# A hand-written order of events, set anew on all five engines, with 270 zero products in place of 390

## The chip, the cores and the metric

The kernel runs on one core of a Trainium2 chip. A core has five engines that each work through their own stream of instructions in order: PE (TensorE, the matrix multiplications), DVE (VectorE), ACT (ScalarE), POOL (GpSimd) and SP (SyncE, which here only issues the DMAs). The engines wait for each other through semaphores. The metric is the time of one execution in microseconds (us) on the device, the median of the runs shown; a profile is one execution more, with a record of every instruction.

## What is computed

A recurrent attention (a delta rule) over 32 independent heads, then a feed-forward network on its output:

```python
B, H, S, D = 4, 8, 768, 48
k_n = k / (np.linalg.norm(k, axis=-1, keepdims=True) + 1e-06)
for t in range(S):
    y[:, :, t] = q_t @ state
    v_old = state^T @ k_n_t
    state = state + beta_t * outer(k_n_t, v_t - v_old)
x = y.transpose(0, 2, 1, 3).reshape(3072, 384)
h = x @ w_in                        # 384 x 2048
g = h * erf(softplus(h))
out = g @ w_out                     # 2048 x 384
```

## The kernel before

**Attention.** The 768 steps are cut into 12 chunks of 64. For each chunk `c` the kernel forms products of keys with keys (`gram_mm ... pg`, masked and scaled in `gram_a`) and of keys with queries (`gram_mm ... pq`, `gram_p`). A triangular system has to be solved for each chunk: the matrix goes to DRAM and back in another layout (`to_dram`, `to_blocks`), 31 rows are eliminated one after the other (`solve_row`, two instructions each, L316 and L318), two chunks at a time; the result goes back through DRAM (`put_blocks`, `from_blocks2`) and is completed by two small products (`merge_t`, `merge_e`, `merge_z`, `merge_m`). The first solve (chunks 0 and 1) runs on DVE, the five others on POOL. Then four recurrences (one per batch entry `b`, index `j = 4c + b`) run through the chunks: `chain_u` on PE, `chain_u2` on DVE, then `chain_s` and `chain_y` on PE, `chain_s2` on DVE, `chain_y2` on ACT.

**Feed-forward.** The output of every chunk makes one group `g` of 256 tokens, so there are 12 groups. The values are scaled and split in two 16-bit parts (`x_max`, `x_all`, `x_scale`, `x_tr`, `x_hi`, `x_lo`), and so are the weights (`w_load`, `w_mask`, `w_sign`, `w_bits`, `w_sum`, then `w_max`, `w_all`, `w_scale`, `w_hi`, `w_lo`, and for `w_in` `w_lo1` on PE and `w_lo2` on ACT). A group has 16 `ffn1` (nine matmuls of 256 columns each, L632), eight units of softplus, erf, product and split (`e_sp`, `e_erf` on ACT, `e_mul` on DVE, `e_split`, `e_rest`), and 16 `ffn2` (six matmuls of 384 columns, L687 to L689). Softplus and erf sit in two table sets of ACT. Where an event needs another set than the event before it in the order, `table` writes a table load (L138).

**Zero products.** `warm` multiplies a tile of zeros by itself, 384 columns, into a bank that nothing reads. `fill` is one such product. 15 are issued at the start, and `WU` more are events of their own.

**What sets the order.** Every call such as `on(us(19), load_q, 0)` puts one event in a list. The list is sorted by the planned time, and then `ORDER`, a tuple written out by hand, picks the events one by one. The instructions of each engine are issued in exactly that order; the scheduler is set to manual for all five engines. An event that isn't ready holds up everything behind it on its engine. So the order on each engine can be read out of the tuple alone.

Around the first solve that gives on PE, before the change: 15 zero products, 5 more, `gram_mm` (1,1,pg), 36 more, three `gram_mm`, 108 more, four `gram_mm` (pq), 7 more, `gram_mm` (2,0,pg), 234 more, `gram_mm` (2,1,pg), `w_all` of `w_in`, `merge_e` of chunk 0. On DVE: the gram products, six `w_sign` and five `w_bits`, the norms of chunks 2 and 3, the 31 solve rows with 10 `w_sign` and 6 `w_bits` between them, four `w_bits`, `gram_a` (2,0), `gram_p` (0,0), `w_max`, `gram_a` (2,1), `merge_t` of chunk 0. SP issues `put_blocks` and `from_blocks2` of both chunks when the solve is done.

Of the kernel before, what the change touches and what calls it, by code (L numbers as in the profile page):

```python
# [11 lines left out]
ALU = mybir.AluOpType  # L12
# [25 lines left out]
C2 = 12.0  # L38
C3 = 16.0
SS2 = 12.8  # L40
S1 = -2.5
SPL = 32
WG = -6
WU = 390
MT = 58
M1 = 0
WL = (0.9, 0.95, 1.0, 1.05, 1.1, 1.15, 24, 24.1, 31.0, 32.5, 34.0, 35.5)
WK = (6.0, 6.7, 7.4, 8.1, 8.8, 9.5, 28, 29, 36.0, 37.5, 39.0, 40.5)
WF = (6.6, 7.3, 8.0, 8.7, 9.4, 10.1, 28.6, 29.6, 36.6, 38.1, 39.6, 41.1)
WI = (17.0, 18.0, 19.0, 20.0, 21.0, 22.0, 31, 32, 50.5, 52.1, 53.7, 55.3)  # L50
# [32 lines left out]
def delta_ffn_kernel(ctx, tc, kT, qT, ktok, vtok, btok, w_in, w_out, cst, out):  # L83
    nc = tc.nc
    te, ve, se, ge, sp = nc.tensor, nc.vector, nc.scalar, nc.gpsimd, nc.sync
# [18 lines left out]
    def on(t, fn, *a, **kw):  # L104
        ev.append((t, len(ev), lambda: fn(*a, **kw)))

    def us(x):
        return (x - T0) / SW
# [279 lines left out]
    ygrp, mg = {}, {}  # L388
# [54 lines left out]
    def chain_y2(j):  # L443
        g, js = divmod(j, GS)
        if js == 0:
            ygrp[g] = []
            mg[g] = sm.tile([P, GS], F32, tag="mg", name=f"mg{g}")
        y = at.tile([P, NP * D], F32, tag="y", bufs=YR, name=f"y{j}")
        ygrp[g].append(y)
        se.copy(y, pcs[j][0][:, :192])  # L450
# [13 lines left out]
    def stage(nm, i, n=RW):  # L464

        return wb[nm].rearrange("p a b -> p (a b)")[:, DM + i * n:DM + i * n + n]
# [32 lines left out]
    def w_bits(nm, i, k):  # L499
        raw = wt[nm]["raw", i]  # L500
        ai = stage(nm, i).bitcast(I32)
        if k == 0:
            ve.scalar_tensor_tensor(ai, ai, 3, raw[:, :, 0], op0=ALU.logical_shift_left, op1=ALU.bitwise_or)
# [202 lines left out]
    def chain_at(j):  # L706
        if j < B:
            return us(MT + 8.3 + 2 * j)
        if j < 2 * B:
            return us(MT + 17 + 2 * (j - B))  # L710
        if j < 3 * B:
            return C2 + 1.2 * (j - 2 * B)
        if j < 4 * B:
            return C3 + 1.2 * (j - 3 * B)
        return j * NFF * SF / GS - NFF * SF - LEAD
# [29 lines left out]
    on(-98, warm, WARM)  # L745
    for i in range(WU):
        on(us(6 + 0.17 * i), fill)
# [8 lines left out]
    for sg in range(2):  # L756
        t = (4, 20)[sg]
# [13 lines left out]
    for c in range(4):  # L771
        t = (5.5, 8, 63.2, 65.2)[c]
# [10 lines left out]
    for c in range(2):  # L783
        for i in range(2):
            t = (56, 57, 71.5, 73)[2 * c + i]
# [3 lines left out]
    for sg in range(NSG):  # L789
# [7 lines left out]
        for s0 in range(31):  # L797
            t = t0 + (t1 - t0) * s0 / 31
# [39 lines left out]
    for j in range(B * NC_):  # L838
        t = chain_at(j)
        d = 1.0 if j >= 2 * B else 2.6 / SW / CS  # L840
        on(t - 3.3 if j >= 2 * B else us(32 + 2 * j) if j < 6 else t - us(6) + us(0), load_v, j)
        on(t - 1.2 if j >= 2 * B else us(52 + 1.3 * j) if j < 6 else t - us(2) + us(0), put_v, j)
        on(t, chain_u, j)
        on(t + 0.2 * d, chain_u2, j)
        if j < B * NC_ - B:
            on(t + CS * d, chain_s, j)
            on(t + (CS + 0.25) * d, chain_s2, j)
        on(t + (CS + 0.05) * d, chain_y, j)
        on(t + (CS + 0.3) * d, chain_y2, j)
        on(t + (CS + 0.7) * d, chain_m, j)  # L850


    for i, (tl, tk, tf, tb) in enumerate(zip(WL, WK, WF, WI)):
        on(us(tl), w_load, "in", w_in.bitcast(I32), i, RI[i])
        on(us(tk), w_mask, "in", i)
        on(us(tf), w_sign, "in", i)
        for k in range(2):
            on(us(tb + 0.8 * k), w_bits, "in", i, k)
        on(us(tb + 2.4), w_sum, "in", i)
    for i in range(NRW):  # L860
        t = us(WOT[i])
        on(t - 0.9, w_load, "out", w_out.bitcast(I32), i, RO[i])
        on(t - 0.3, w_mask, "out", i)
        on(t - 0.2, w_sign, "out", i)
        for k in range(2):
            on(t + 0.15 * k, w_bits, "out", i, k)
        on(t + 0.5, w_sum, "out", i)
# [52 lines left out]
    ev.sort(key=lambda e: (e[0], e[1]))  # L920
    if ORDER:
        ev = [ev[i] for i in ORDER]
    E = mybir.EngineType
# [45 lines left out]
```

## Time and profile before

| what | value |
|---|---|
| three runs | 699.67, 704.69 and 709.21 us, median 704.69 |
| profiled execution, its own time | 704.84 us |
| span of its instructions | 703.1 us |
| mean granted clock of TensorE | 0.977 |
| PE busy | 674.4 us, of which 69.9 are the 405 zero products |
| ACT busy | 542.9 us, of which 234.8 are 183 table loads |
| DVE and POOL busy | 424.3 and 307.6 us |

The span runs from the first to the last instruction; the execution's own time has 1.74 us around it. Matmuls are pipelined: the record of one lasts longer than the pace at which they follow one another (405 records of 337 ns on the mean, but 69.9 us of busy time). "PEclk" in a row is the granted clock of TensorE as a share of full speed.

### The profile page before, as it was taken

To read this page: it belongs to the slowest core of one execution; us is meant where nothing else is said; L and a number is where in the kernel's file an instruction comes from. 1 tells how busy PE (TensorE), PEld (TensorE's weight loads), DVE (VectorE), ACT (ScalarE), POOL (GpSimd) and SP (SyncE) were. 2 spreads that over 40 slices of the span, in tenths; PEclk is the share of its full clock that TensorE was granted. 3 is DMA by queue.
4 is the path that set the end of the run, shared out by engine and by line. 5 is a ranking of instruction groups with operands and counts; after the bars stand their busy time and mean duration, and the time that the engine had idled before them with its cause. 6 is when DMAs were issued, how large, how long until landed. Compare 5 with 4: busy or idle time off the path is not lost.

```text
span 703.1 us, 22184 instructions
## 1 busy us (share of the span) xinstructions
PE 674.4 (96%) x9473; PEld 509.3 (72%) x9473; DVE 424.3 (60%) x976; ACT 542.9 (77%) x767; POOL 307.6 (44%) x492
## 2 busy tenths in 40 slices
PE   8999888899999999999999999999999999999997
PEld 4666575666777777777786877777777778777764
DVE  3769586696656975568665668565554645534321
ACT  7333234998998599879688796798897897899994
POOL 2012004798379718981276851288612131111111
PEclk9999968999999999999999999999999999999999
DMA  9692539403633166123461152521230400101000
GB/s 319 152 296 86 121 91 275 119 1 91 132 64 82 24 154 138 35 60 80 92 158 25 37 132 46 106 60 33 49 91 12 82 14 2 25 1 25 1 23 22
DMA packets 87395, 59.05 MB, mean 84 GB/s; under 512 B 67776, under 2 KB 77120, under 8 KB 87296
## 3 DMA queue, kind: packets, MB, share of 16 engines
q1 hardware_dynamic: 87296, 57.63, 32.9%
q8 instruction: 74, 1.21, 0.7%
q14 instruction: 25, 0.20, 0.1%
HBM read 43.45 MB, written 14.16 MB: 82 GB/s over the span
## 4 chain that ended last, share of the span: by engine, by line
PE 68%; ACT 15%; DVE 10%; issue 3%; DMA 2%; SPq 1%; ACTq 0%; DVEq 0%
PE ph L632 19%; PE warm L153 9%; PE pr L687 7%; ACT L138 7%; PE pr L689 6%; PE pr L688 6%; PE pq L255 3%; PE pc L441 3%; PE pg L255 3%; PE pc L414 3%; ACT L L659 2%; ACT L L654 2%; PE pc L427 2%; DVE z L435 2%; PE pr L558 1%
## 5 line engine op out<-in xcount | busy, mean ns | idle before, releaser
L138 ACT ACT_TABLE_LOAD x183 | 234.8, 1283 | 4.0 <-PEq L962 0.7
L632 PE MATMUL ph<-xh,w_in 128*128 128x256 f16 x1152 | 219.2, 275 | 4.1 <-DVE L L663 4.0
L632 PEld LDWEIGHTS <-w_in 128*128 128x128 f16 x1728 | 167.2, 99 | 42.8 <-issue 6.6
L676 POOL TENSOR_TENSOR H<-L,H 128x512 f16<-128x512 f32 x58 | 67.4, 1163 | 213.9 <-DVE H L672 144.2
L632 PE MATMUL ph<-xl,w_in 128*128 128x256 f16 x576 | 158.4, 275 | 0.0
L687 PE MATMUL pr<-w_out,H 128*128 128x384 f16 x384 | 125.7, 327 | 0.0
L689 PE MATMUL pr<-w_out,H 128*128 128x384 f16 x384 | 125.4, 326 | 0.0
L688 PE MATMUL pr<-w_out,H 128*128 128x384 f16 x384 | 125.3, 326 | 0.0
L663 DVE SCALAR_TENSOR_TENSOR L<-ph,L 128x512 f32<-128x512 f32 x96 | 65.8, 686 | 84.5 <-ACT L L659 83.8
L401 POOL TENSOR_TENSOR z<-v,nm 64x192 f32<-64x192 f32 x96 | 50.8, 529 | 101.3 <-DMA v<-vtok 54.9
L316 POOL TENSOR_TENSOR tmptmpg<-gb,xb 128x31 f32<-128x31 f32 (+15 forms) x155 | 82.9, 535 | 24.1 <-DMA gb<-d 15.1
L318 POOL TENSOR_TENSOR xb<-xb,tmptmpg 128x31 f32<-128x31 f32 (+15 forms) x155 | 86.7, 559 | 12.2
L654 ACT ACTIVATE L<-ph,xct 128x512 f32<-128x512 f32 x96 | 66.0, 687 | 17.6 <-PE ph L632 14.5
L153 PE MATMUL warm<-zero 128*128 128x384 f16 x405 | 69.9, 337 | 1.1 <-DVE zero L144 1.1
L153 PEld LDWEIGHTS <-zero 128*128 128x128 f16 x405 | 40.3, 101 | 29.1 <-issue 3.4
L659 ACT ACTIVATE L<-L 128x512 f32<-128x512 f32 x96 | 60.3, 630 | 1.0
L689 PEld LDWEIGHTS <-H 128*128 128x128 f16 x384 | 37.5, 98 | 24.9
L687 PEld LDWEIGHTS <-H 128*128 128x128 f16 x384 | 37.5, 98 | 17.5
L420 DVE TENSOR_TENSOR z<-pc,ga 64x192 f32<-64x192 f32 x88 | 31.2, 354 | 29.9 <-PE pc L414 25.1
L688 PEld LDWEIGHTS <-H 128*128 128x128 f16 x384 | 37.6, 98 | 15.6
L670 ACT CAST H<-L 128x512 f16<-128x512 f32 x56 | 34.3, 614 | 17.1 <-DVE L L663 16.8
L435 DVE TENSOR_TENSOR z<-pc,z 48x192 f32<-48x192 f32 x80 | 28.2, 352 | 28.1 <-PE pc L441 27.2
(139 smaller groups left out, 948.0 us busy)
## 6 DMA issues: line engine op xcount, KB each, us to landing
raw_in<-w_in SPq DMA_DIRECT2D x12, 512.0 KB, 7.0
raw_out<-w_out SPq DMA_DIRECT2D x12, 512.0 KB, 5.9
d<-A SPq DMA_DIRECT2D x22, 256.0 KB, 3.1
k<-ktok SPq DMA_DIRECT2D x12, 384.0 KB, 4.9
kpg<-kT SPq DMA_DIRECT2D x24, 192.0 KB, 4.9
qp<-qT SPq DMA_DIRECT2D x24, 192.0 KB, 4.0
v<-vtok SPq DMA_DIRECT2D x48, 96.0 KB, 2.6
out<-ob SPq DMA_DIRECT2D x48, 96.0 KB, 2.2
```

The lines of the kernel that those rows point to most:

```text
L138: se.add_instruction(mybir.InstLoadActFuncSet(name=nc.get_next_instruction_name(), act_func_set_id=i, ins=[], outs=[]))
L153: te.matmul(wp[0], zero[:, :P], zero, start=True, stop=True)
L316: eng.tensor_tensor(tv, G[:, s, s + 1:].unsqueeze(1).broadcast_to([P, ncol, nr]), Xv[:, :, s:s + 1].broadcast_to([P, ncol, nr]), op=ALU.mult)
L318: eng.tensor_tensor(Xv[:, :, s + 1:], Xv[:, :, s + 1:], tv, op=ALU.add)
L632: te.matmul(ph, w[:, i, kt * P:kt * P + P], G[x][:, :, ksl], start=(m == 0), stop=(m == 8))
L654: se.activation(unit(g, u), G["ph", u], AF.Softplus, bias=0.0, scale=G["ct"])
L659: se.activation(Lu, Lu, AF.Erf, bias=0.0, scale=1.0)
L663: ve.scalar_tensor_tensor(Lu, fg[g]["ph", u], HSC, Lu, op0=ALU.mult, op1=ALU.mult)
L676: (ve if u % (2 if g < GLE else GLM) == 0 else ge).tensor_tensor(G["gl", u], unit(g, u), G["gh", u], op=ALU.subtract)
L687: te.matmul(G["po"][a], gh[:, o, asl], wout_h[:, i, :], start=(i == 0), stop=False)
L688: te.matmul(G["po"][a], gh[:, o, asl], wout_l[:, i, :], start=False, stop=False)
L689: te.matmul(G["po"][a], gl[:, o, asl], wout_h[:, i, :], start=False, stop=(i == NFF - 1))
```

## The change

`WU` goes from 390 to 270, so 120 of the zero products fall away. `ORDER` is another permutation of all the events: on each engine nearly every event has another neighbour. `chain_y2` is rewritten so that the members of a group can come in any order, and the second, empty call of `w_bits` is dropped from the list (it issued nothing). No other instruction is added or taken away by hand; the number of table loads follows from the order.

```diff
-ORDER = (0,1,3,4,2,27,5,6,7,8,9,12,10,11,22,24,13,25,28,30,14,60,15,236,34,
...
+ORDER = (0,1,2,12,7,21,22,24,25,28,30,34,36,37,40,42,44,45,49,51,33,27,3,5,
...
-WU = 390
+WU = 270
...
-        if js == 0:
-            ygrp[g] = []
+        if g not in ygrp:
+            ygrp[g] = {}
...
-        ygrp[g].append(y)
+        ygrp[g][js] = y
...
-    def w_bits(nm, i, k):
+    def w_bits(nm, i):
...
-        if k == 0:
-            ve.scalar_tensor_tensor(ai, ai, 3, raw[:, :, 0], op0=ALU.logical_shift_left, op1=ALU.bitwise_or)
+        ve.scalar_tensor_tensor(ai, ai, 3, raw[:, :, 0], op0=ALU.logical_shift_left, op1=ALU.bitwise_or)
```

The new tuple, read out as the order on each engine up to the first feed-forward work (F and a number: so many zero products; `s` a `solve_row`):

```
PE    warm 15, pg(0,0), F14, pg(0,1), pg(1,0), pg(1,1), F133, pq(1,1), F7,
      pq(0,1), pq(0,0), F21, pg(2,0), pq(1,0), F69, pg(2,1), pg(3,1), F18,
      merge_e 0, F5, merge_z 0, merge_e 1, chain_u 0, pg(3,0), merge_z 1,
      chain_u 1, chain_y 0, merge_m(1,1), chain_s 0, merge_m(1,0), chain_s 1,
      chain_u 2, chain_u 3, w_all in, chain_y 1, chain_s 2, chain_y 3,
      chain_y 2, chain_s 3, chain_u 5, x_tr(0,0), F3, w_lo1 0, chain_y 5,
      w_lo1 1, 2, 3, x_all 0, w_lo1 4, chain_s 5, chain_u 4, w_lo1 5,
      x_tr(0,1), w_lo1 6, pq(2,0), w_lo1 7, ffn1 2, 0, 1, ...
DVE   norm_sum 2, 0, 1, norms of chunks 0 and 1, norm_sum 3, gram_a(0,0),
      gram_a(0,1), w_sign x2, w_bits, gram_a(1,0), gram_a(1,1), then 5 w_sign,
      6 w_bits and the norms of chunks 2 and 3, s0 to s30 with 11 w_sign and
      5 w_bits between them, w_ident, gram_p(1,1), gram_p(1,0), w_sign x2,
      w_bits x2, gram_a(2,0), gram_a(2,1), merge_t 0, gram_p(0,1),
      merge_e2(0,0), merge_t 1, gram_p(0,0), merge_z2(0,0), ...
SP    kT 0, k 1, beta 0, k 2, k 0, w in8, kT 1, w out0, k 3, w out2, in2, in1,
      out11, in4, to_dram 0, 1, to_blocks 0, beta 1, to_blocks 1, w in5, in7,
      in0, out3, out1, q 1, w out10, v 0, q 0, w in6, kT 2, w in10, cst,
      from_blocks 0, w in11, in9, in3, out5, kT 3, w out6, v 2, kT 2, w out4,
      put_blocks 0, 1, from_blocks 1, v 1, from_blocks2 0, 1, ...
```

After that the order goes on as before in kind, with the two `ffn1` of a unit next to each other, the softplus of a unit often set directly ahead of another unit's, and the feed-forward work of a group spread over a longer stretch. Counted over the whole tuple, the ACT order switches its table set 147 times, where the old one switches 183 times.

More of the change, by code (lines that the diff above doesn't have):

```diff
@@ L856, in delta_ffn_kernel @@
         on(us(tf), w_sign, "in", i)
-        for k in range(2):
-            on(us(tb + 0.8 * k), w_bits, "in", i, k)
+        on(us(tb), w_bits, "in", i)
         on(us(tb + 2.4), w_sum, "in", i)
@@ L864, in delta_ffn_kernel @@
         on(t - 0.2, w_sign, "out", i)
-        for k in range(2):
-            on(t + 0.15 * k, w_bits, "out", i, k)
+        on(t, w_bits, "out", i)
         on(t + 0.5, w_sum, "out", i)
```

2 lines of the change are left out of this document (1 added, 1 removed).

## The prediction, made before the changed kernel was run

> **What bounds the kernel now.** I read the busy shares first, then busy time by stage, then the timeline where a stage has holes.
>
> ```profile
> span 703.1 us, 22184 instructions
> PE 674.4 (96%) x9473; PEld 509.3 (72%) x9473; DVE 424.3 (60%) x976; ACT 542.9 (77%) x767; POOL 307.6 (44%) x492
> L138 ACT ACT_TABLE_LOAD x183 | 234.8, 1283 | 4.0 <-PEq L962 0.7
> L153 PE MATMUL warm<-zero 128*128 128x384 f16 x405 | 69.9, 337 | 1.1 <-DVE zero L144 1.1
> ...
> 0.00:86.10 86.10, 81.23 (x729) 51.10 (x730) 56.74 (x149) 32.48 (x63) 13.15 (x24) 0.98 0.67 194
> 86.10:160.00 73.90, 61.61 (x1072) 47.80 (x1073) 57.65 (x139) 51.59 (x107) 38.86 (x60) 0.83 0.46 121
> 160.00:698.00 538.00, 531.59 (x7676) 410.37 (x7674) 309.45 (x690) 458.80 (x598) 255.61 (x409) 1.00 0.27 61
> 698.00:703.10 5.10, 0.00 (x0) 0.00 (x0) 0.48 (x1) 0.00 (x0) 0.00 (x0) 0.90 0.32 77
> ```
>
> The columns of the stage rows are: stage, length, busy time of PE, weight loads, DVE, ACT and POOL, granted clock, DMA share, GB/s. From 160 to 698 us PE is busy 531.59 of 538 at full clock, with work that the change keeps: at most 6.4 us can be gained there, whatever the other engines do. What can be won lies before 160. Up to 86.1 us PE is busy too, but 69.9 of 81.23 us are zero products; the work that counts there is the first solve on DVE. From 86.1 to 160 PE has 12.3 us of holes and a clock of 0.83.
>
> ```profile
> 18.73 0.69 DVE L265 TENSOR_TENSOR A<-pg,gn 128x512 f32<-128x512 f32 x1 [2.28 <-PE pg L255]
> 21.21 0.68 DVE L265 TENSOR_TENSOR w_out<-pr,gn 128x512 f32<-128x512 f32 x1
> 33.17 0.19 DVE L316 TENSOR_TENSOR tmpT<-gb,xb 128x31 f32<-128x31 f32 x1
> 47.76 0.43 DVE L497 TENSOR_SCALAR raw_out<-raw_out 128x512 int32<-128x512 int32 x1 [3.73 <-DMA raw_out<-w_out]
> 51.54 0.43 DVE L497 TENSOR_SCALAR raw_out<-raw_out 128x512 int32<-128x512 int32 x1 [0.91 <-DMA raw_out<-w_out]
> 70.88 0.21 DVE L318 TENSOR_TENSOR xb<-xb,tmpT 128x31 f32<-128x31 f32 x1
> 71.12 1.09 SPq L323 DMA_DIRECT2D d<-xb  x2
> 74.20 4.30 SPq L338 DMA_DIRECT2D xm<-d  x8
> xm<-d SPq DMA_DIRECT2D x48, 64.0 KB, 2.4
> 44.34 38.20 PE L153 MATMUL warm<-zero 128*128 128x384 f16 x234
> 82.47 1.15 PE L255 MATMUL pg<-kpg 48*64 48x64 f32 x32
> 83.66 0.69 DVE L265 TENSOR_TENSOR A<-pg,gn 128x512 f32<-128x512 f32 x1 [8.08 <-PE pg L255]
> 84.27 1.42 DVE L345 STREAM_TRANSPOSE T<-xm 32x512 f32<-32x512 f32 x2
> 86.07 1.20 PE L353 MATMUL pe<-T,A 32*32 32x32 f32 x64 [1.17 <-DVE m_in L520]
> ```
>
> The solve runs from 33.17 to 71.09. Its result leaves at 71.12, and the loads back into `xm` are issued from 74.20 on, chunk 0 in the first half of the 4.30 us, so chunk 0 is there at about 74.20 + 2.15 + 2.4 = 78.75. But `merge_t` (L345) starts at 84.27: on DVE it stands behind `gram_a` (2,1), which waited 8.08 us for a `gram_mm` that stood behind 234 zero products on PE, done at 82.5. So **the zero products have become the end of the stage**: they hold the merge by 84.27 - 78.75 = 5.5 us.
>
> **The change part by part.**
>
> *Fewer zero products ahead of the merge.* The old order has 390 and the 15 of the start ahead of `merge_e` 0, the new one 262 and the 15. One costs 38.20/234 = 0.163 us, so the queue ahead of the merge is 128 x 0.163 = 20.9 us shorter. This isn't the gain: the solve's end then decides. What becomes of the 5.5 us: in the new order the last gram products of chunks 2 and 3 are followed by 18 zero products, 2.9 us. If the keys of chunk 3 land by 60 us, as the DMA order allows, PE is through at about 66, and the hold is gone: -5.5. Bound on the other side: 0, if PE's queue is late again.
>
> *An earlier start of the solve.* The last `gram_a` ahead of the solve began at 21.21, after a wait of 2.28 for a `gram_mm` behind 36 zero products, and after six `w_sign` and a `w_bits`. In the new order `gram_mm` (0,0) comes first, and two `w_sign` and one `w_bits` stand in between; against that, one more norm sum stands ahead (I allow 1 us). I get 20.4 for the end, against 21.89. Behind it DVE has 5 `w_sign`, 6 `w_bits` and 18 norm instructions:
>
> ```profile
> 15.69 0.76 DVE L497 TENSOR_SCALAR raw_in<-raw_in 128x512 int32<-128x512 int32 x2
> 22.47 3.10 DVE L503 SCALAR_TENSOR_TENSOR w_in<-w_in,raw_in 128x512 int32<-128x512 int32 x5
> 29.00 0.18 DVE L215 TENSOR_SCALAR n<-n 128x32 f32<-128x32 f32 x1
> L316 DVE TENSOR_TENSOR tmpT<-gb,xb 128x31 f32<-128x31 f32 (+15 forms) x31 | 11.5, 372 | 0.8
> L318 DVE TENSOR_TENSOR xb<-xb,tmpT 128x31 f32<-128x31 f32 (+15 forms) x31 | 11.4, 368 | 1.1
> ```
>
> 5 x 0.38 + 6 x 0.62 + (33.17 - 29.00) = 9.8, so the solve starts at about 30.3, 2.9 earlier. (The trip of the matrix through DRAM took at most 33.17 - 21.89 = 11.3 before; if it takes that, 31.7.)
>
> *A solve with fewer waits.* Rows: 11.5 + 11.4 + 1.9 between instructions = 24.8. Before there were 10 `w_sign` and 6 `w_bits` in it and 4.6 us of waits for weights (3.73 + 0.91); 37.9 in all. The new order has 11 and 5, which is about the same work. Its waits I bound from 0 to 5: the SP order has `w in6` stuck until ACT has freed a buffer, and ACT stands in `w_mask` of out10, which SP loads after out3 and out1; so `w in3` comes late, by my count about 1 us after DVE needs it. I take 1.3, so -3.3. The solve then ends near 30.3 + 37.9 - 3.3 = 64.9, and `merge_e` 0 begins at about 64.9 + 7.6 (the trip back, as 78.75 against 71.12) + 1.5 = 74.0, in place of 86.07: **-12.1 us**, bounds -17 and -6.
>
> *From the merge to the first softplus.*
>
> ```profile
> 134.82 0.69 ACT L654 ACTIVATE L<-ph,xct 128x512 f32<-128x512 f32 x1
> 89.86 0.68 DVE L358 COPY T<-pe 32x512 f32<-32x512 f32 x1
> 127.06 1.09 DVE L620 SCALAR_TENSOR_TENSOR xl<-pt,xsx,xh 128x256 f16<-128x256 f32 x3 [0.24 <-ACT xh L615]
> 89.86:128.15 38.29, 32.84 (x713) 27.06 (x713) 28.88 (x69) 18.40 (x43) 9.98 (x22) 0.76 0.70 185
> 134.80:160.00 25.20, 21.07 (x215) 14.41 (x213) 20.00 (x52) 24.88 (x50) 22.77 (x34) 0.92 0.07 18
> ```
>
> This took 134.82 - 86.07 = 48.75 us. No engine fills it: in the 38.29 us from the first evacuation of the merge to the last split of `x`, DVE is busy 28.88, ACT 18.40. It is a chain of short steps with waits between them. The new DVE list for the same stretch has about the same work (one `chain_u2`, one `chain_s2` and five `w_sign` fewer, one `w_bits`, the scale of `w_in` and a norm sum more), but starts earlier after `merge_e` (two transposes and two masks, 2.8 us, stood in front of both evacuations; now only one mask does), and takes recurrences 4, 6 and 7 behind the first `ffn1`. Stepping through it by hand I get the first softplus 37.5 us after `merge_e` 0 without a hitch, 48.75 if nothing improves. I take 41: **-7.8**.
>
> After the first softplus ACT fills the time up to 160 (24.88 of 25.20), with the same work in both orders. So what is gained up to there is handed on in full.
>
> *The long stretch.* Table loads go from 183 to 147: 36 x 1.283 = 46 us of ACT's time. In a stretch in which PE is the bound I cost that at nothing: PE's 531.59 us cover it. It would be worth something only where PE waits for ACT's products, within the 6.4 us. Against it, the new order sets consumers closer. Counting PE's work between `chain_u` and its first consumer, from chunk 3 on: 18 of 36 have under 2 us, before it was 4. In between, `chain_u2` needs two instructions on DVE:
>
> ```profile
> L420 DVE TENSOR_TENSOR z<-pc,ga 64x192 f32<-64x192 f32 x88 | 31.2, 354 | 29.9 <-PE pc L414 25.1
> L663 DVE SCALAR_TENSOR_TENSOR L<-ph,L 128x512 f32<-128x512 f32 x96 | 65.8, 686 | 84.5 <-ACT L L659 83.8
> PE ph L632 <- DVE L L663: 2.6, 3, 1.3
> ```
>
> 2 x 0.354 plus the way there and back is about 1 us if DVE is free; with one wide instruction (0.686) in front, PE waits about half a microsecond. 14 places more x 0.4 = 5.6 lost, against 2.6 that PE waits today for `e_mul`, which I take as halved: **+4**. Bounds -6.4 (no holes at all) and +14.
>
> *The rest.* `chain_y2` and `w_bits` issue what they did before: 0. The tail (5.1 us after PE's last product) is the same.
>
> Sum, from this execution's own 704.84: -12.1 - 7.8 + 4 = -15.9, which gives 689. The median of the runs is 704.69, so the two stand together.
>
> **The rivals.**
>
> *A cold clock in the merge.* In the new order PE is through its queue at about 66 and the merge begins at 74.
>
> ```profile
> 88.00:90.00 2.00, 0.00 (x0) 0.50 0.84 250
> 98.00:100.00 2.00, 2.00 (x40) 0.50 0.00 0
> 102.00:104.00 2.00, 2.00 (x86) 1.00 0.04 8
> ```
>
> (Columns here: stage, length, PE busy, granted clock, DMA share, GB/s.) Before, the clock stood at 0.50 in rows from 88 to 100, after idle time, and at 1.00 again from 102. The new order could be at half speed from the first merge product on and stay so, since only 8 zero products stand between `merge_e` 0 and the first `ffn1`. The 32.84 us that PE was busy in the stretch from 89.86 to 128.15, at 0.76, are 25 at full speed and 50 at half. With the clock as low as before the stretch is no shorter than it was, which gives 689 + 7.8 = 697; at half throughout it is 50 - 38.29 = 12 us longer still, 709. I put it at 700.
>
> The Trainium skill, "TensorE: Matmul & The Clock Gate", Part 1, has this as its rule: half clock by default, full after a busy window of about 3.4 us, and back to half after an idle one. The trace agrees with two levels, 0.50 and 1.00; by that rule taking zero products out speaks against the change. Against the rival: before, the stretch had 0.76 on the mean with no zero product in it at all.
>
> *The long stretch gives it back.* Each of the 18 short gaps waits for a wide instruction in full: 18 x 0.686 = 12.3 in place of 4, so 697.
>
> *Slower.* The same place, but DVE behind: if PE stood 2 us at each of the 18 gaps, and at the second consumer again, that is 72 us of stalls; from 34 us of them on (0.95 at each of 36) the kernel is slower than 719. It needs DVE to be one to two wide instructions late at every one of them, at a DVE share of 309.45/538 = 58%.
>
> *The merge comes no sooner.* If loads in the new SP order hold the solve by 7 us more, it ends at 72, and only the hold of 5.5 and the shorter front remain: 704.8 - 5.5 - 7.8 + 4 = 695.5.
>
> **How the numbers follow.** I give the forecast 0.58 (its own range 676 to 694), the cold clock 0.15, the long stretch that gives back 0.12, the late solve 0.08, slower 0.07. The predicted time is 689. 2% of 704.69 is about what a measurement of this kernel can tell from no change, so faster means under 690.6 and slower over 718.8. Of the forecast's 0.58 some 0.05 lies above 690.6; a few hundredths of the others lie below. That makes 0.55 faster, 0.38 within, 0.07 slower. The range takes in the rivals up to 700 and the bound of the long stretch above them, and below the better ends of the solve and of the front: 673 to 704.
>
> **What would show it.** In the profile after, `merge_e` 0 begins at about 74 (hold and solve right) and the first softplus at about 115 (front right); DVE's waits for `raw_out` inside the solve fall from 4.6 to under 2; no `gram_a` waits 8 us for PE; PE is busy to within 8 to 12 us from the first steady stage to its last product; table loads are 147. I am wrong if PE's idle time after 150 grows by more than 15 us, if the first softplus comes later than 125, or if the solve ends after 70.

## The result, and the profile after

The changed kernel takes 660.42 us (median of 4 runs, 658.36 to 664.21), against 705.24 for the kernel before on the same chip (4 runs, 699.67 to 709.21). The ratio is 0.9376, with a 95% interval of 0.9297 to 0.9455. So it is faster by 6.2%, where 2.2% were forecast, and 660.42 lies below the range.

The page of the kernel after: span, busy shares, the chain that ended last by engine and by line, and two groups of instructions (line, form, count, busy time and mean ns of one, idle time before). Line numbers behind `w_bits` are one to three lower than before: `ffn1` is L631, softplus L653, erf L658, `e_mul` L662.

```profile
span 662.4 us, 21898 instructions
PE 639.5 (97%) x9353; PEld 493.6 (75%) x9353; DVE 415.7 (63%) x976; ACT 491.2 (74%) x731; POOL 309.5 (47%) x492
PE 73%; DVE 10%; ACT 7%; DMA 4%; POOL 2%; issue 2%; SPq 1%; DVEq 0%; POOLq 0%; ACTq 0%
L138 ACT ACT_TABLE_LOAD x147 | 188.6, 1283 | 3.3 <-PEq L959 0.7
L153 PE MATMUL warm<-zero 128*128 128x384 f16 x285 | 52.6, 347 | 1.1 <-DVE zero L144 1.1
```

In the page of before, the chain that ended last had this share by engine:

```profile
PE 68%; ACT 15%; DVE 10%; issue 3%; DMA 2%; SPq 1%; ACTq 0%; DVEq 0%
```

Where the time went can be read from three points. First the timeline of after, for the solve, the merge and the first softplus (start, duration, engine, line, operation; in brackets the idle time before it and what ended it):

```profile
30.58 0.19 DVE L316 TENSOR_TENSOR tmpT<-gb,xb 128x31 f32<-128x31 f32 x1
38.18 0.43 DVE L497 TENSOR_SCALAR raw_out<-raw_out 128x512 int32<-128x512 int32 x1 [1.13 <-DMA raw_out<-w_out]
58.36 0.43 DVE L497 TENSOR_SCALAR raw_in<-raw_in 128x512 int32<-128x512 int32 x1 [4.75 <-DMA raw_in<-w_in]
64.58 0.43 DVE L497 TENSOR_SCALAR raw_out<-raw_out 128x512 int32<-128x512 int32 x1 [1.18 <-DMA raw_out<-w_out]
66.64 0.21 DVE L318 TENSOR_TENSOR xb<-xb,tmpT 128x31 f32<-128x31 f32 x1
74.23 1.43 DVE L345 STREAM_TRANSPOSE T<-xm 32x512 f32<-32x512 f32 x2 [1.32 <-DMA xm<-d]
76.90 1.20 PE L353 MATMUL pe<-T,A 32*32 32x32 f32 x64
114.57 0.69 ACT L653 ACTIVATE L<-ph,xct 128x512 f32<-128x512 f32 x1
```

Then busy time by stage. The first row is before, from the first softplus to PE's last product. The other three are after: the merge to the first softplus, that same long stretch, and its part from 160 us on (stage, length, busy time of PE, weight loads, DVE, ACT and POOL with their counts, granted clock, DMA share, GB/s):

```profile
134.80:697.80 563.00, 552.63 (x7889) 424.78 (x7886) 329.32 (x740) 483.52 (x647) 278.38 (x442) 0.99 0.26 59
...
76.90:114.60 37.70, 35.69 (x714) 28.70 (x714) 29.76 (x73) 27.23 (x61) 21.28 (x40) 0.86 0.61 151
114.60:657.20 542.60, 538.45 (x8013) 423.04 (x8010) 329.12 (x751) 432.46 (x612) 279.77 (x437) 1.00 0.27 63
160.00:657.00 497.00, 496.16 (x7398) 390.99 (x7395) 293.63 (x672) 390.45 (x540) 249.34 (x392) 1.00 0.28 63
```

| part, in the profiled executions | before | after | difference | forecast |
|---|---|---|---|---|
| up to `merge_e` 0 | 86.07 | 76.90 | -9.2 | -12.1 |
| `merge_e` 0 to the first softplus | 48.75 | 37.67 | -11.1 | -7.8 |
| first softplus to PE's last product | 563.0 | 542.6 | -20.4 | +4 |
| what follows, with the time around the span | 7.0 | 7.0 | 0 | 0 |
| sum | 704.84 | 664.21 | -40.6 | -15.9 |

The profiled execution of after is the slowest of its four, so the medians lie 4 us further apart than this table says.

The reader is to see two things. Up to the first softplus the sum came out, by two misses that cancel: 114.57 us where about 115 was written down. All of the miss in the total lies behind it. In that stretch PE does 124 matmuls **more** than before (8013 against 7889, since some work now comes later; at the pace of the rows these are worth about 2.7 us), and yet it is busy 14.2 us less (552.63 to 538.45) and idle 6.2 us less (563.00 - 552.63 = 10.37 to 542.60 - 538.45 = 4.15). From 160 on it is idle for 0.84 us of 497. That PE can be busy less with the same work is what the prediction had ruled out.

### The profile page after: what moved, and what is told of

Read it like the earlier page. It is cut to its first block, busy times and chain, and to the rows that moved or that the text cites. A ratio compares the mean times of both kernels' runs of the same rounds, so it can differ in the third digit from the quotient of the medians.

```text
span 662.4 us, 21898 instructions
## 1 busy us (share of the span) xinstructions
PE 639.5 (97%) x9353; PEld 493.6 (75%) x9353; DVE 415.7 (63%) x976; ACT 491.2 (74%) x731; POOL 309.5 (47%) x492
## 4 chain that ended last, share of the span: by engine, by line
PE 73%; DVE 10%; ACT 7%; DMA 4%; POOL 2%; issue 2%; SPq 1%; DVEq 0%; POOLq 0%; ACTq 0%
PE ph L631 24%; PE pr L686 9%; PE pr L687 8%; PE pr L688 8%; PE pc L441 3%; PE pc L414 3%; DMA raw_out<-w_out 3%; PE pm L379 3%; PE pg L255 2%; PE pq L255 2%; PE pc L427 2%; PE pz L366 2%; ACT L138 2%; PE pe L353 2%; ACT w_out L541 1%
## 5 line engine op out<-in xcount | busy, mean ns | idle before, releaser
L631 PE MATMUL ph<-xh,w_in 128*128 128x256 f16 x1152 | 206.7, 273 | 0.0
L138 ACT ACT_TABLE_LOAD x147 | 188.6, 1283 | 3.3 <-PEq L959 0.7
L631 PEld LDWEIGHTS <-w_in 128*128 128x128 f16 x1728 | 166.1, 98 | 28.1 <-issue 0.9
L631 PE MATMUL ph<-xl,w_in 128*128 128x256 f16 x576 | 157.1, 273 | 0.0
L675 POOL TENSOR_TENSOR H<-L,H 128x512 f16<-128x512 f32 x58 | 69.5, 1209 | 175.6 <-DVE H L671 122.9
L662 DVE SCALAR_TENSOR_TENSOR L<-ph,L 128x512 f32<-128x512 f32 x96 | 65.8, 688 | 102.2 <-ACT L L658 93.9
L401 POOL TENSOR_TENSOR z<-v,nm 64x192 f32<-64x192 f32 x96 | 53.2, 555 | 132.7 <-DMA v<-vtok 111.0
L653 ACT ACTIVATE L<-ph,xct 128x512 f32<-128x512 f32 x96 | 65.9, 687 | 58.3 <-PE ph L631 51.2
L318 POOL TENSOR_TENSOR xb<-xb,tmptmpg 128x31 f32<-128x31 f32 (+15 forms) x155 | 86.6, 559 | 12.1
L316 POOL TENSOR_TENSOR tmptmpg<-gb,xb 128x31 f32<-128x31 f32 (+15 forms) x155 | 80.7, 521 | 13.0 <-DMA be<-btok 3.2
L658 ACT ACTIVATE L<-L 128x512 f32<-128x512 f32 x96 | 59.3, 628 | 0.9
L688 PEld LDWEIGHTS <-H 128*128 128x128 f16 x384 | 37.5, 98 | 25.2 <-issue 0.4
L153 PE MATMUL warm<-zero 128*128 128x384 f16 x285 | 52.6, 347 | 1.1 <-DVE zero L144 1.1
L686 PEld LDWEIGHTS <-H 128*128 128x128 f16 x384 | 37.5, 98 | 20.7
L153 PEld LDWEIGHTS <-zero 128*128 128x128 f16 x285 | 28.7, 103 | 21.9 <-issue 4.7
L255 PE MATMUL pg<-kpg 48*64 48x64 f32 x736 | 28.0, 230 | 8.3 <-DVE qp L276 4.7
```

What stands on the lines that cost most here:

```text
L138: se.add_instruction(mybir.InstLoadActFuncSet(name=nc.get_next_instruction_name(), act_func_set_id=i, ins=[], outs=[]))
L153: te.matmul(wp[0], zero[:, :P], zero, start=True, stop=True)
L316: eng.tensor_tensor(tv, G[:, s, s + 1:].unsqueeze(1).broadcast_to([P, ncol, nr]), Xv[:, :, s:s + 1].broadcast_to([P, ncol, nr]), op=ALU.mult)
L318: eng.tensor_tensor(Xv[:, :, s + 1:], Xv[:, :, s + 1:], tv, op=ALU.add)
L631: te.matmul(ph, w[:, i, kt * P:kt * P + P], G[x][:, :, ksl], start=(m == 0), stop=(m == 8))
L653: se.activation(unit(g, u), G["ph", u], AF.Softplus, bias=0.0, scale=G["ct"])
```

## The experiments

Two theories stood at the start. **T1**: the long stretch is shorter by its own order (the neighbours of each product on PE, and the place of the table loads on ACT). **T2**: what is gained early is only handed on, and the long stretch is shorter because of what was moved across its start, or because of the zero products. Ratios are to the kernel before, on the same chip, with the 95% interval.

**1. The hold alone (old_270).** The old order, with the last 120 zero products ahead of `gram_mm` (2,1,pg) taken out.

```diff
 ORDER, read out: gram_mm (2,0,pg)
-fill x234
+fill x114
 gram_mm (2,1,pg)
-WU = 390
+WU = 270
```

> The order of before on all engines, without the last 120 of the 234 zero products that stood ahead of the last gram product: nothing else differs. Theory that they held the merge: the merge begins about 5.5 us sooner (at about 80.5 in place of 86.1) and the time falls to about 699. Rival, the clock: fewer zero products leave TensorE cold, the stretch from the merge to the first softplus grows by 3 to 8 us and the time is 700 to 708. Rival, the number of zero products is what counts (120 x 0.163 = 19.6 us): 685.

Measured: 698.56 us, ratio 0.9924 (0.9898 to 0.9950). Its timeline around the merge:

```profile
76.42 0.69 DVE L265 TENSOR_TENSOR A<-pg,gn 128x512 f32<-128x512 f32 x1 [0.58 <-PE pg L255]
...
77.21 1.43 DVE L345 STREAM_TRANSPOSE T<-xm 32x512 f32<-32x512 f32 x2
...
79.02 1.91 PE L353 MATMUL pe<-T,A 32*32 32x32 f32 x64 [1.05 <-DVE m_in L519]
```

The last `gram_a` waits 0.58 us in place of 8.08, the merge starts at 79.02 in place of 86.07, and the kernel is 5.5 us shorter: the hold was real. The merge came 7.0 us sooner and not 5.5; of these, 5.3 are left at the first softplus (129.52 in place of 134.82). So that the kernel gained just the 5.5 that was read from the rows is partly luck.

**2. and 3. Each half of the order (front_new, front_old).** `front_new` takes the new order up to `chain_y` of recurrence 4 and then the rest in the old order. `front_old` takes the old order up to the first softplus and then the rest in the new one.

```diff
-ORDER = old
+ORDER = new, up to chain_y(4); then the events that are left, as in old
...
-ORDER = old
+ORDER = old, up to e_sp(0, 0); then the events that are left, as in new
```

> The new order up to and with chain_y of recurrence 4 (about the first softplus), all that is left in the old order. Theory that the long stretch is shorter because of its own new order: the first softplus comes at about 115 as with the new order, but the rest takes as long as before (563 us from there to the last product), so 684 to 688. Rival, that the long stretch only profits from a better start: the time is near 662.

> The old order up to and with the first softplus, all that is left in the new order. Theory of the long stretch's own order: the first softplus at about 135 as before, then 543 to 546 us to the last product, so 683 to 687. Rival, the better start: 700 to 705.

Measured: 688.79 us, ratio 0.9785 (0.9761 to 0.9808), and 685.31 us, ratio 0.9730 (0.9686 to 0.9773). `front_new` has its first softplus at 110.5 and a long stretch of 571.8 us, 8.8 more than before: part of what the front won is lost where the two orders meet (PE waits 5.38 us for a load of queries at 125.1). `front_old` has its first softplus at 133.4, about where it was, and then (busy time by stage, from there to PE's last product):

```profile
133.40:674.20 540.80, 534.56 (x7895) 420.45 (x7894) 324.04 (x740) 432.50 (x611) 281.57 (x441) 1.00 0.27 62
```

With the front of before and all but the same number of matmuls (7895 against 7889), PE is busy 18.1 us less and the stretch is 22.2 us shorter. (The profiled execution took 681.21 us, so a few us of this may be chance.) T2 falls as far as what was moved across the start goes: the long stretch has a gain of its own.

**4. No zero products (new_nofill).** The new order without its 270 zero products; the 15 at the start stay.

```diff
 ORDER: every fill left out
-WU = 270
+WU = 0
```

> The new order without any of the 270 zero products (the 15 of the start stay). Theory that they only stand in TensorE's idle time and cost and bring little: the merge begins where it did (76 to 78), the time is 659 to 664. Rival, the clock: without them TensorE is at half clock from the start to the merge and in the merge, the first softplus is 4 to 10 us later, the time 664 to 671. Rival, they stand on the path: 650 to 656.

Measured: 660.89 us, ratio 0.9392 (0.9352 to 0.9433). That can't be told from the changed kernel, although the mean granted clock falls from 0.980 to 0.940. The zero products neither cost nor bring anything here, and with that the rest of T2 falls. From the merge to the first softplus PE is busy at half clock for 14.4 us in place of 9.5, and the stretch is 38.2 us long in place of 37.7. The Trainium skill, "TensorE: Matmul & The Clock Gate", Part 1, has half clock as the default state and full clock only behind a busy window. The trace agrees on the state (the clock does fall); a cost in time does not show in this kernel.

**5. and 6. More changes of kind on PE (new_alternate, new_alternate2).** Here is what the neighbours of a product cost. The timeline of PE alone, first before, then after (start, duration, line, form, count; records overlap, so starts are to be read):

```profile
400.59 0.67 PE L441 MATMUL pc<-z,qp 128*64 128x48 f32 x16
401.19 1.20 PE L353 MATMUL pe<-T,A 32*32 32x32 f32 x64
402.32 0.67 PE L414 MATMUL pc<-z,xm 128*64 128x48 f32 x16
402.93 0.28 PE L632 MATMUL ph<-xh,w_in 128*128 128x256 f16 x1
...
407.73 0.27 PE L632 MATMUL ph<-xh,w_in 128*128 128x256 f16 x1
407.93 1.20 PE L366 MATMUL pz<-xm,T 32*32 32x32 f32 x64
```

```profile
400.97 1.14 PE L414 MATMUL pc<-z,xm 128*64 128x48 f32 x32
401.94 1.20 PE L441 MATMUL pc<-z,qp 128*64 128x48 f32 x32
403.07 1.28 PE L427 MATMUL pc<-z,k 64*48 64x48 f32 x48
404.29 0.67 PE L441 MATMUL pc<-z,qp 128*64 128x48 f32 x16
...
410.60 0.33 PE L688 MATMUL pr<-w_out,H 128*128 128x384 f16 x1
410.76 0.27 PE L631 MATMUL ph<-xh,w_in 128*128 128x256 f16 x1
...
412.62 0.27 PE L631 MATMUL ph<-xh,w_in 128*128 128x256 f16 x1
412.73 0.27 PE L597 MATMUL pt<-ident,y 128*128 128x128 f32 x1
```

Before, a `chain_u` (L414, 16 matmuls) stands alone between products of other shapes and takes 402.93 - 402.32 = 0.61 us. After, two of them stand together and take 401.94 - 400.97 = 0.97, 0.49 each. The last matmul of an `ffn1` before a 32x32 product takes 0.20 (407.73 to 407.93); before another 128x128 product it takes 0.11, even where that one is 32-bit (412.62 to 412.73). From `ffn2` to `ffn1` nothing is added (0.16, the pace within `ffn2`). So it is a change of the array's shape that costs, about 0.09 us each; the pace within a kind is nearly the same in both kernels (from start to start, before and after: 30.0 and 29.5 ns for one matmul of `chain_u`, 109.6 and 109.4 for `ffn1`). Counted by kind of product in the tuple, the old order has 304 changes behind the first `ffn1` and the new one 231, because it puts chain products of two or three recurrences side by side. But not each of these changes the shape: the last matmul of a `chain_s` takes 0.04 us ahead of a `merge_m`, which has its shape, and 0.14 ahead of a `chain_y`. Counted by shape from the records of the long stretch (128x128, 128x64, up to 64x64, and 32x32, with the transposes of `x` among the first), there are 257 changes before, 156 after and 146 in `front_old`. The two kernels put changes back into the new order, by letting `chain_s` and `chain_y` alternate and by placing an `ffn2` between neighbouring `chain_u`.

```diff
 ORDER, read out, for instance:
-chain_s(j) chain_s(j+1) chain_y(j) chain_y(j+1)
+chain_s(j) chain_y(j) chain_s(j+1) chain_y(j+1)
...
-chain_u(j) chain_u(j+1)
+chain_u(j) ffn2(n) chain_u(j+1)
```

> The new order, but on TensorE the chain_s and chain_y of a chunk alternate, and some ffn2 are set between neighbouring chain_u: 281 changes of the kind of product after the first ffn1 in place of 231 (the old order has 304), the same products otherwise. Theory that each change of kind costs TensorE about 0.095 us in the long stretch: its full-speed time from the first softplus to the last product grows from 538.5 by 4.7 to about 543, the kernel from 660.5 to about 665. Rival, that TensorE is shorter for other reasons (better start, fewer waits): full-speed time within 1 us of 538.5, kernel 659 to 662.

> As the earlier kernel with alternating products, but no chain_y passes the load of the next queries (in the earlier kernel some did, so that they read the queries of another chunk and TensorE waited for these loads): 277 changes of kind after the first ffn1 in place of 231. Theory of 0.095 us for a change: TensorE's full-speed time from the first softplus to the last product is 538.5 + 4.4 = 542.9 and the kernel 664 to 666. Rival: full-speed time within 1 us of 538.5 and the kernel 659 to 662.

`new_alternate` (281 changes of kind): 676.53 us, ratio 0.9614 (0.9584 to 0.9645). Some of its `chain_y` stand behind the load of the next chunk's queries, read those, and made PE wait for the load; so it computes something else and its time isn't that of the alternation alone, and `new_alternate2` keeps them ahead of the load. `new_alternate2` (277 changes of kind, 203 of shape, so 46 or 47 more than the changed kernel): 672.54 us, ratio 0.9547 (0.9518 to 0.9576), 12 us more than the changed kernel where 4 to 6 were expected. Its long stretch, and what PE waited for in it that after did not (us in all, times, longest):

```profile
114.40:667.30 552.90, 546.01 (x8013) 426.31 (x8010) 326.88 (x752) 432.99 (x612) 281.54 (x438) 0.99 0.27 62
```

```profile
PE ph L631 <- DVE L L662: 2.4, 2, 1.5
```

The part that was to be measured came out. With the time at half clock counted half, PE's busy time is 542.8 us against 538.5 in after: 4.3 more for 46 changes, 0.093 each. But idle time grew by 2.7 us and half clock by 6.3 us, which costs 3.1, and neither was expected. The half clock need not be the alternation's doing: it begins at 133.4, behind two waits (1.41 and 0.51 us) that the changed kernel has there too (1.06 and 0.54), without a fall. A product that comes later by a few hundred ns can also delay whoever waits for it; which delays made the waits wasn't tried separately.

**7. Table loads back in (new_tables).** The new order with 32 more table loads in groups 2 to 11, 16 ahead of a softplus and 16 ahead of an erf, so 179 in place of 147. They load the set that is loaded already and change nothing else.

```diff
-    def table(i):
-        if ts[0] != i:
+    def table(i, again=False):
+        if ts[0] != i or again:
...
-        table(SET_ERF)
+        table(SET_ERF, (g, u) in ((2, 0), (2, 1), (3, 0), ...))
```

> The new order with 32 table loads of ACT put back in (179 in place of 147, spread over groups 2 to 11, each loads the set that is already there). Theory that ACT is covered by TensorE in the long stretch: 660 to 662, TensorE idle there at most 2 us more. Rival, that the fewer table loads are what took TensorE's waits away (10.4 us of idle time before, 4.1 after): 664 to 670.

Measured: 671.97 us, ratio 0.9547 (0.9517 to 0.9577), 11.5 us more than the changed kernel, 0.36 for each load, and more than the rival's 664 to 670. Its long stretch and PE's longest kind of wait:

```profile
111.60:666.70 555.10, 543.67 (x8013) 424.95 (x8010) 327.63 (x751) 474.97 (x644) 281.52 (x439) 0.99 0.27 62
```

```profile
PE ph L631 <- DVE L L662: 6.8, 7, 1.7
```

One of these waits, in the timeline of the same kernel:

```profile
258.88 1.28 ACT L138 ACT_TABLE_LOAD   x1
260.17 0.63 ACT L658 ACTIVATE L<-L 128x512 f32<-128x512 f32 x1
260.81 1.28 ACT L138 ACT_TABLE_LOAD   x1
262.10 0.63 ACT L658 ACTIVATE L<-L 128x512 f32<-128x512 f32 x1
262.76 0.69 DVE L662 SCALAR_TENSOR_TENSOR L<-ph,L 128x512 f32<-128x512 f32 x1 [2.93 <-ACT L L658]
...
263.51 0.28 PE L631 MATMUL ph<-xh,w_in 128*128 128x256 f16 x1 [1.75 <-DVE L L662]
```

A load of 1.28 us stands between two erfs that follow one another. The second erf, its `e_mul` on DVE and, behind that, the next `ffn1` on PE are late. `ffn1` waits for `e_mul` because `e_mul` is the last reader of the PSUM bank that this `ffn1` writes, and there are two such banks. So PE waits 1.75 us, while ACT is busy for 474.97 of 555.10 us and PE for 543.67. PE's idle time grew from 4.15 to 11.43 us, and 6.8 of it are such waits. (Some 3.3 us of this profile are half clock at 130.5 to 137.4, ahead of the first added load at 222. The 11.5 us doesn't hang on that: its two runs with a mean clock of 0.984 and 0.985 took 670.5 and 670.9 us, the changed kernel's two at 0.985 took 658.4 and 659.2.) PE, 98% busy, does not hide ACT's work: the way from `ffn1` over softplus, load, erf and `e_mul` back to the bank is short of slack in places, and there a load counts in full. On the mean it costs 0.36 of its 1.28 us. The Trainium skill, "ScalarE: Activation LUTs", section "What ACT_TABLE_LOAD costs", adds a drain of about 1380 ns to a load of about 1283; the trace agrees on 1283 but not on the drain: the load at 258.88 does change the set, and the erf starts 0.01 us after its end (258.88 + 1.28 against 260.17).

**8. Two loads of weights moved (new_late_sign).** The new order, with the `w_sign` of `in3` and `out6`, which waited for their DMAs inside the solve, moved behind it on DVE.

```diff
 ORDER, read out: solve_row ...
-w_sign(in, 3) ... w_sign(out, 6) ... last solve_row
+... last solve_row, w_sign(out, 6), w_sign(in, 3)
```

> The new order with two w_sign (w_in part 3, w_out part 6) moved from between the solve rows to behind the solve: these waited 4.75 and 1.18 us for their loads. Theory that the solve sets the merge and the merge the end: the solve ends near 61 in place of 66.9, the merge begins 4 to 6 us sooner and the time falls to 655 to 657. Rival, the loads then hold the next w_sign or the merge's own way, or the front gives it back later (w_scale of w_in needs these parts): 659 to 661.

Measured: 659.13 us, ratio 0.9357 (0.9325 to 0.9389). The solve ended at 58.6 in place of 66.9, but one of the two moved waits only changed its place: it now stands on DVE between the solve and `merge_t`.

```profile
66.49 0.43 DVE L497 TENSOR_SCALAR raw_out<-raw_out 128x512 int32<-128x512 int32 x1 [4.87 <-DMA raw_out<-w_out]
```

Of 8.2 us, 5.7 are left at `merge_e` 0 (71.2 in place of 76.9) and 4.3 at the first softplus (110.26). `merge_e` 0 also began at 72.5 in `new_nofill`, which has the `w_sign` where they were. A gain of 1.3 us isn't told from none here, so the 3 to 5 us expected of it weren't shown.

**9. Fewer loads in the old order (old_pairs).** In groups 2 to 6, 18 erfs with all that follows them are moved behind the next softplus, so that two softplus and two erfs share a load: 147 loads in the old order as well.

```diff
 ORDER, read out:
-e_sp(g, u) e_erf(g, u) e_mul(g, u) ... e_sp(g, u+1) e_erf(g, u+1)
+e_sp(g, u) ... e_sp(g, u+1) e_erf(g, u) e_mul(g, u) e_erf(g, u+1)
```

> The old order with 390 zero products, changed only in that in groups 2 to 6 the erf (and what hangs on it) of 18 units is set behind the softplus of the next unit: 147 table loads in place of 183, as many as the new order has; TensorE's own order is the old one. Theory that ACT is so close to TensorE in the long stretch that table loads cost time (32 more cost the new order 11 us): TensorE's idle and half-clock time after the first softplus (10.4 and 6.8) falls and the kernel takes 693 to 700. Rival, that a delayed erf holds the PSUM bank that the next ffn1 needs: TensorE waits for e_mul more than 2.6 us, and the time is 703 to 715.

Measured: 741.91 us, ratio 1.0542 (1.0514 to 1.0571). PE's waits for `e_mul`, and one of them:

```profile
PE ph L631 <- DVE L L662: 27.3, 18, 2.5
```

```profile
259.06 0.27 PE L631 MATMUL ph<-xh,w_in 128*128 128x256 f16 x1
259.37 0.69 ACT L653 ACTIVATE L<-ph,xct 128x512 f32<-128x512 f32 x1 [2.06 <-PE ph L631]
260.08 1.28 ACT L138 ACT_TABLE_LOAD   x1
261.37 0.63 ACT L658 ACTIVATE L<-L 128x512 f32<-128x512 f32 x1
262.03 0.69 DVE L662 SCALAR_TENSOR_TENSOR L<-ph,L 128x512 f32<-128x512 f32 x1 [3.58 <-ACT L L658]
...
262.78 0.28 PE L631 MATMUL ph<-xh,w_in 128*128 128x256 f16 x1 [2.47 <-DVE L L662]
```

ACT has 46 us less to do and the kernel is 38 us slower, far beyond the rival's 703 to 715. Two softplus need both banks filled before the first erf can start. PE has nothing to write to until softplus, load, erf and `e_mul` are through, 262.78 - 259.37 = 3.4 us; ACT itself had waited 2.06 us for PE. Behind the first softplus PE is idle for 38.6 us in place of 10.4, and at half clock for 23.9 us in place of 6.8. The number of loads as such is not what counts: a pair gains only if PE has other work while both banks are held. That the new order has such work there, with its chain and `ffn2` products grouped, fits its 147 loads without one wait of `ffn1` for `e_mul`, but wasn't tried by itself.

**10. Less work for ACT in the old order (old_split_dve).** 40 `e_split` of groups 2 to 11 run on DVE in place of ACT.

```diff
-SPA = (0, 2, 4, 6)
+SPA = ()
```

> The old order with 390 zero products, but the 40 e_split that ACT does in groups 2 to 11 (about 0.6 us each, 24 us) are done by DVE at the same places of the order; table loads stay at 183. Theory that ACT's load in the long stretch costs time: 695 to 701. Rival, that it is the place of the table loads and not ACT's load, or that DVE is then late in its turn: 703 to 712.

Measured: 702.89 us, ratio 0.9991 (0.9975 to 1.0008). The long stretch:

```profile
134.10:693.90 559.80, 549.96 (x7888) 424.13 (x7886) 346.53 (x780) 460.85 (x606) 281.46 (x442) 1.00 0.26 60
```

ACT is busy 22.7 us less than before in it (460.85 against 483.52), at no gain that can be measured. PE's busy time, 549.96 of 559.80 us, stays nearly what it was (552.63 of 563.00). So in the old order less work for ACT brings nothing by itself. But the work went to DVE: PE's waits for `e_mul` fell from 4.0 us to 1.6, and its waits for what DVE makes for `chain_u` rose from 0.4 to 2.6. What a lighter ACT would bring with DVE as it was, this run doesn't show.

## Why the prediction was wrong

**Right: the zero products were the end of the stage.** Experiment 1 takes the hold away by itself and gives -5.5 us of time, with the merge 7.0 sooner.

**Right to some tenths: the earlier start of the solve.** It begins at 30.58, where 30.3 was forecast, so 2.6 us earlier and not 2.9.

**Wrong: "a solve with fewer waits", -3.3.** The waits for weights inside the solve did not fall from 4.6 us to 1.3, they rose to 7.1 (1.13, 4.75 and 1.18 in the timeline). The one for `w in3`, foreseen as about 1 us, is the 4.75. That the solve was still 1.65 us shorter (36.27 in place of 37.92) comes from its work: DVE is busy for 27.66 us of it in place of 30.77, and why its instructions took less isn't shown. The solve ended at 66.85 in place of 64.9, and the trip back took 10.05 us in place of 9.1. `merge_e` 0 came at 76.90, so the whole step was -9.2 and not -12.1. Of this size, though, not much can be made: in the five other profiles with the new order up to there (one of them without zero products) the wait for `w in3` is 2.1 to 6.1 us, and `merge_e` 0 begins at 72.5 to 77.4, and the 74.0 lies in that span.

**Mis-sized the other way: "from the merge to the first softplus", -7.8.** Stepping through the order by hand had given 37.5 without a hitch, and 41 was taken to be careful. It was 37.67, and 36.7 to 38.2 in the five other profiles. The two errors cancel: the first softplus was forecast at 115 and came at 114.57, which is luck. The rival of a cold clock fell: PE's clock was 0.86 on the mean there, and 38.2 us were enough with no zero products at all.

**Wrong: "the long stretch", +4, where the chip showed -20.4.** Three sentences of that step failed.

- "At most 6.4 us can be gained there, whatever the other engines do." This took PE's busy time for a constant of its work. By the two stage rows it fell by 14.2 us. Of these 3.4 are half clock that went (6.8 us before, by the clock's records, none after, counted half), and 10.8 are at full clock. Experiment 6 prices a change of the array's shape at 0.093 us, and the new order has 101 fewer (257 to 156), which is 9.4 us. Since the stretch of after also has the 2.7 us of additional products, some 4 us stay open. `front_old`, with the products of before to within six, says the same: 18.1 us less, of which 3.4 are half clock and 10.3 the 111 fewer changes. For the rest there are candidates (x transposes that waited among the `chain_u`, waits so short that overlapping records hide them), but they weren't tried one by one. The Trainium skill, "TensorEngine Tiling (Array Packing)", section "Key Properties", says that a change of tiling mode, and not of the tile alone, drains TensorE. The trace agrees that such a change costs, as the rows of experiment 5 show, and that what keeps the shape doesn't; that it is a drain, no run here shows. The price is that of this case.
- "I cost that at nothing: PE's 531.59 us cover it", of the table loads. Experiment 7 shows that a load on the way from `ffn1` back to its bank is not covered: 0.36 us each on the mean. The chain that ended last in before had pointed there, with ACT at 15% (7% in after), and the prediction passed it over. Experiments 9 and 10 set the limit of this: fewer loads, or work moved from ACT to DVE, bring nothing in the old order.
- "14 places more x 0.4 = 5.6 lost", for the short gaps between `chain_u` and its consumers. This did not occur; no run shows the 0.4 us. From 160 us on PE is idle for 0.84 us, all waits together. DVE was in time, busy 293.63 of 497 us.

The idle time of the long stretch fell by 6.2 us. Before, 4.0 of it were waits for `e_mul` and some 2.4 waits of `w_lo1` for `w_hi`, as these rows of before show (the list of PE's waits; three of the four `w_lo1` waits lie behind the first softplus, one of 1.14 ahead of it):

```profile
PE ph L632 <- DVE L L663: 4.0, 4, 1.3
PE pr L559 <- ACT w_in L542: 3.6, 4, 1.4
```

Neither is in the list of after. How much of that comes from 36 fewer loads and how much from the rest of the order was not separated.

So a gain was forecast, for half of its reasons: in the changed kernel the part up to the first softplus and the part behind it each brought about 20 us, and the second was not in the sum.

## What to carry to other kernels

A PE that is over 95% busy is not at its least time: read the start-to-start times at the seams between products of different shapes, count the seams, and see what an order with fewer would save (here 0.093 us each). And ask of the other engines not how busy they are, but how long a buffer of PE stays held: with two banks, a load of 1.28 us between product and release is paid in places although PE is 98% busy. Zero products that keep the clock up are worth a look by taking them out: here some of them held a queue for 5.5 us in the old order, and in the new one all 270 moved nothing.

## What the runs showed that was not expected

- A change of the array's shape on PE costs about 0.09 us: the last `ffn1` matmul took 0.20 in place of 0.11 ahead of a 32x32 product, the last `ffn2` matmul 0.26 in place of 0.16 ahead of any smaller one, and 46 more changes lengthened PE's busy time by 4.3 us. A change from 16-bit to 32-bit within 128x128 cost nothing that shows (0.11).
- The clock can fall after short waits, but doesn't always. Before, PE waited 0.58 and 1.33 us in the 2.2 us up to 159.2 and ran at 0.59 and 0.55 in the next 4 us; in the run with more table loads it waited 1.75 us up to 263.5 and stayed at 1.00. What decides it, these runs don't show. These rows are before, then that run (stage, length, busy times, clock as above):

```profile
159.00:161.00 2.00, 1.76 (x9) 1.27 (x9) 2.00 (x5) 1.98 (x5) 1.47 (x3) 0.59 0.00 0
161.00:163.00 2.00, 2.00 (x12) 1.50 (x10) 2.00 (x3) 1.28 (x1) 1.95 (x2) 0.55 0.00 0
```

```profile
264.00:266.00 2.00, 2.00 (x30) 1.66 (x29) 1.72 (x6) 0.49 (x2) 1.76 (x4) 1.00 0.00 0
```

- 262 zero products ahead of the merge and 8 behind it raised the mean granted clock from 0.940 to 0.980, and the time stayed the same (660.89 and 660.42 us).
- One and the same order gives solves of different length. With the same instructions up to the merge, DVE waited from 2.5 us (`new_tables`) to 6.1 us (`new_alternate2`) for the same load of weights, and the first softplus came at 110.5 to 115.1 us.
